# Retention and softplus feed-forward on one core: the second pass's second layer by the seven-product scheme, its out weights' sums earlier, and the order of a group's state sums kept by GpSimd

## Chip, cores and metric

One core of a Trainium2 chip. The metric is the device time of one execution in microseconds; before the change the median of three runs is 844.63 us (844.49 to 847.51).

## What is computed

Retention over 8 batches, 8 heads, 576 positions and 64 features, then a feed-forward layer over the 4608 tokens, all in float32:

```python
scores = scale * np.matmul(q, k.transpose(0, 1, 3, 2))
ret = scores * Dmat[None, :, :, :]            # Dmat: gamma_h ** (i - j) for i >= j, else 0
x = np.ascontiguousarray(attn_out.transpose(0, 2, 1, 3)).reshape(B * S, H * D)      # 4608 x 512
h = x @ w_in                                  # 512 x 2048
g = np.maximum(h, 0.0) + np.log1p(np.exp(-np.abs(h)))
return (g @ w_out).astype(np.float32)         # 2048 x 512
```

## The kernel before, in words

Every float32 product of the feed-forward is made of three TensorE products of parts (a head and a rest, `TERMS`, line 54): each operand is split by a ScalarE copy into its head and a VectorE subtraction into its rest.

The 4608 tokens are nine units of 512. Unit 0 is worked in the opening, which also splits the weights. Then come four passes over two units each (units 1 and 2, 3 and 4, 5 and 6, 7 and 8), counted in the code by `s` from 0 to 3, and called here the first to the fourth pass. The 2048 hidden features are 16 pieces of 128 or 8 pairs `J` of pieces.

- **First layer.** In passes two to four, and for pairs 6 and 7 of the first, two units and two pieces are one 2x2 block product by the Strassen-Winograd scheme: seven block products (`product`, line 820, six matmuls each; matmul line 830) in place of eight. The sums of weights that it needs (`sums_dram`) are made in the first pass. The rest of the first pass is plain: `plain_slot` (line 836), 12 slots `p` for unit 1 and 12 for unit 2, each with 12 matmuls of line 830 and 12 of the second layer.
- **Second layer.** `FULL = 2` (line 62): in the first two passes it is plain (`output_mm`, line 482: 12 matmuls for each piece of each unit, 384 in a pass). The second unit's hidden values are parked in DRAM (`kept`) and worked after the pairs (`kept_parts`). In the third and fourth pass the second layer goes by seven products too: `full_pair` (line 1129) makes two of them beside the first layer (`second`, line 1113, six matmuls at line 1117), and `full_phase` (line 1221) the other five after the eighth pair, 8 x 6 matmuls each: 336 in a pass.
- **Out weights' sums.** For these, eight pairs of out weights are added up (`whole_out`, line 625: two VectorE additions of 128x512), combined (`combine_out`, line 631: four VectorE operations of 128x256), split (`combine_split`: two ScalarE copies, two VectorE subtractions) and stored (1 MB). Pairs 0 to 6 go through this in the second pass's pairs (`extras`), pair 7 in the third pass. The raw out weights are stored in the second pass's kept part (lines 1088 to 1090).
- **Ring.** All weights of `product` and `second` come from DRAM through a ring of five 256 KB buffers (`block_load`, line 588, order in `order`, line 576). Each product frees one and issues the load of the fifth block after it. All DMAs are issued by SyncE (SP), in program order.
- **Retention.** Two steps of 128 tokens at a time (a group) are put into the slots and pairs: `chunk_products` (line 303) issues up to 128 small matmuls in four batches (`together`): state sums with t = 0 beside scores, scores beside values, values beside the cross products, and the cross products beside the state sums with t = 1. Both halves of the state sums write the same PSUM bank (`third`) from two row groups of TensorE. That the first half is done before the second begins is ensured by `mark` (line 336): a VectorE copy of one column of the first half, on which the second half waits.
- **GpSimd** scales the loaded values of the next group (`scale_values`, line 197, after the DMA `qv`), copies and scales the state (lines 259 and 278), and makes the sums of x for the next pass (`start_combined`, lines 434 to 437: four operations of 128x256) in slots 3, 5, 7 and 9 of unit 1 and 6, 8, 10 and 11 of unit 2. Groups stand in slots 0, 2, 4, 6, 8 of unit 1, in pairs 6 and 7, in the odd slots of unit 2, and in all pairs of passes two and three.

The program's order is that of the code on each engine; tables of numbers (`schedule` and `job`) put the preparations into slots and pairs. In a full pair the jobs of pair J run on VectorE in pair J + 1 (`last_difference`), after the split of its first hidden block and before the group's masking.

## Time and profile before

| | |
|---|---|
| median of 3 runs | 844.63 us |
| the profiled execution | 844.79 us |
| its span, first to last instruction | 843.0 us |
| TensorE matmuls busy | 829.7 us (98%) |
| VectorE, ScalarE, GpSimd busy | 602.4, 536.2, 157.5 us |
| DMA engines' mean busy share, rate | 72.6%, 242 GB/s |

A matmul's busy time is modelled and overlaps the next; so six matmuls of a product are shown as 1.52 us, although the next product starts 1.36 us after them. A break is therefore about 0.16 us longer than the idle time that a row shows. VectorE rows tell what each operation takes, and in square brackets what ended an idle time before it.

### The profile page before, as it was taken

Reading aid. Unit: us, or ns where it says so; the run is one execution under the profiler, and the core shown is the slowest. Engines: PE = TensorE matmul, PEld = TensorE weight load, DVE = VectorE, ACT = ScalarE, POOL = GpSimd, SP = SyncE. Lnnn points to the kernel's source line nnn. Section 1 sums busy time; section 2 is a strip of 40 time slices with the busy share of each in tenths; the row PEclk is TensorE's granted clock in tenths of the full one; section 3 lists DMA queues with packets and bytes.
Section 4 is the critical chain, followed back from the end, with each engine's and each line's share of the span. In section 5 each row is a group of like instructions: output and inputs, shape, how many; then the busy total and the mean of one; then the engine's idle time right before and its main releaser. Section 6 shows DMA issues by size and latency. Waiting matters only on the chain.

```text
span 843.0 us, 18984 instructions
## 1 busy us (share of the span) xinstructions
PE 829.7 (98%) x7370; PEld 674.8 (80%) x7370; DVE 602.4 (71%) x1024; ACT 536.2 (64%) x921; POOL 157.5 (19%) x212
## 2 busy tenths in 40 slices
PE   7999999999999999999999999999999999999998
PEld 6788888887888888888888888787778888888786
DVE  5999965876587667777775744877789955555875
ACT  6778754447654447667766436676775658878643
POOL 4322222440222441111101000112110002212100
PEclk9999999999999999999999999999999999999999
DMA  9898878656677763988789747879756676666665
GB/s 364 299 304 307 289 259 311 224 197 225 227 258 261 253 206 105 325 277 268 252 282 305 271 176 243 255 218 302 226 155 213 209 243 191 188 192 194 198 205 190
DMA packets 137481, 203.64 MB, mean 242 GB/s; under 512 B 10288, under 2 KB 99888, under 8 KB 137392
## 3 DMA queue, kind: packets, MB, share of 16 engines
q1 hardware_dynamic: 137392, 202.43, 72.6%
q8 instruction: 59, 0.97, 0.5%
q14 instruction: 30, 0.25, 0.1%
HBM read 156.25 MB, written 46.14 MB: 240 GB/s over the span
## 4 chain that ended last, share of the span: by engine, by line
PE 85%; DVE 5%; ACT 4%; DMA 3%; issue 1%; POOL 1%; SPq 0%; DVEq 0%; POOLq 0%; ACTq 0%
PE y L482 23%; PE acc L830 18%; PE sum L1117 12%; PE two L830 11%; PE h L453 4%; PE third L830 4%; PE third L220 2%; PE two L204 2%; PE two L1117 1%; PE two L282 1%; PE third L1117 1%; PE acc L1117 1%; DMA ring<-combined 1%; PE two L294 1%; DMA raw<-whole 1%
## 5 line engine op out<-in xcount | busy, mean ns | idle before, releaser
L482 PE MATMUL y<-wout,g 128*128 128x512 f32 x960 | 233.7, 392 | 0.2 <-DVE g L475 0.2
L482 PEld LDWEIGHTS y<-wout,g 128*128 128x128 f32 x960 | 178.5, 188 | 38.7 <-PE h L453 0.6
L830 PE MATMUL acc<-xt,ring 128*128 128x512 f32 x768 | 194.1, 391 | 0.4 <-DMA ring<-combined 0.2
L830 PEld LDWEIGHTS acc<-xt,ring 128*128 128x128 f32 x768 | 143.6, 188 | 32.7 <-ACT parts L1107 0.7
L830 PE MATMUL two<-xt,ring 128*128 128x512 f32 x480 | 122.4, 391 | 1.3 <-DVE quad L956 0.5
L1117 PE MATMUL sum<-parts,ring 128*128 128x512 f32 x480 | 118.1, 396 | 0.0
L830 PEld LDWEIGHTS two<-xt,ring 128*128 128x128 f32 x480 | 89.6, 188 | 22.0 <-ACT ab L1154 1.6
L1107 ACT CAST parts<-g 128x512 fp32r<-128x512 f32 x112 | 68.5, 621 | 60.0 <-PE sum L1117 19.4
L1117 PEld LDWEIGHTS sum<-parts,ring 128*128 128x128 f32 x480 | 89.1, 188 | 21.7 <-DMA ring<-outsplit 0.6
L1111 DVE TENSOR_TENSOR parts<-g,parts 128x512 fp32r<-128x512 f32 x112 | 78.0, 714 | 29.9 <-ACT parts L1107 28.6
L462 ACT ACTIVATE ab<-ab 128x512 f32<-128x512 f32 x128 | 81.0, 632 | 4.1
L463 ACT ACTIVATE ab<-ab 128x512 f32<-128x512 f32 x128 | 80.9, 632 | 4.1
L471 ACT CAST g<-ab 128x512 fp32r<-128x512 f32 x60 | 37.1, 619 | 57.5 <-DVE ab L467 35.8
L197 POOL TENSOR_TENSOR qv<-qv,consts_sb 128x256 f32<-128x256 f32 x61 | 45.7, 749 | 125.5 <-DMA qv<-others 125.5
L475 DVE TENSOR_TENSOR g<-ab,g 128x512 fp32r<-128x512 f32 x60 | 44.2, 737 | 16.2 <-ACT g L471 15.3
L259 POOL COPY sx<-s 64x256 f32<-64x256 f32 (+1 forms) x34 | 13.2, 389 | 207.6 <-PE third L220 161.2
L1127 DVE SCALAR_TENSOR_TENSOR g<-g,ab 128x512 f32<-128x512 f32 x64 | 45.2, 716 | 7.3 <-ACT ab L463 7.1
L453 PE MATMUL h<-xt,win 128*128 128x512 f32 x192 | 48.3, 400 | 1.0 <-DVE x L397 0.7
L278 POOL TENSOR_TENSOR s<-s,consts_sb 128x256 f32<-128x256 f32 (+1 forms) x31 | 20.3, 656 | 127.8 <-DVE s L276 111.7
L453 PEld LDWEIGHTS h<-xt,win 128*128 128x128 f32 x192 | 35.4, 188 | 9.6 <-ACT wout L563 0.8
L1213 POOL TENSOR_TENSOR g<-g 128x512 f32<-128x512 f32 x9 | 12.3, 1369 | 151.2 <-DVE g L1127 151.2
L461 ACT ACTIVATE ab<-quad 128x512 f32<-128x512 f32 x40 | 25.2, 631 | 23.4 <-DVE quad L956 12.0
(182 smaller groups left out, 1322.5 us busy)
## 6 DMA issues: line engine op xcount, KB each, us to landing
ring<-split SPq DMA_DIRECT2D x126, 256.0 KB, 3.9
ring<-combined SPq DMA_DIRECT2D x104, 256.0 KB, 3.6
qv<-others SPq DMA_DIRECT2D x61, 320.0 KB, 4.8
wst<-w SPq DMA_DIRECT2D x32, 512.0 KB, 5.8
ring<-outcombined SPq DMA_DIRECT2D x64, 256.0 KB, 3.4
keys<-others SPq DMA_DIRECT2D x61, 256.0 KB, 4.8
ring<-outsplit SPq DMA_DIRECT2D x48, 256.0 KB, 3.8
split<-win SPq DMA_DIRECT2D x16, 512.0 KB, 6.5
```

The source lines that it names most:

```text
L197: nc.gpsimd.tensor_mul(v, v, f.unsqueeze(2).broadcast_to([P, 4, D]))
L453: nc.tensor.matmul(h, wins[p][:, a, kt * P:(kt + 1) * P], xt[:, b, T1 + kt // 2, kt % 2], start=(n == 0), stop=(n == 3 * NKT - 1))
L462: nc.scalar.activation(ab, ab, AF.Exp, scale=-1.0)
L463: nc.scalar.activation(ab, ab, AF.Ln, bias=1.0)
L471: nc.scalar.copy(g[:, HI], ab)
L475: nc.vector.tensor_sub(g[:, LO], ab, g[:, HI].bitcast(F32))
L482: nc.tensor.matmul(ys[u][tt], g[:, a, tt * P:(tt + 1) * P], wouts[p][:, b], start=(p == 0 and n == 0), stop=(p == NF - 1 and n == 2))
L830: nc.tensor.matmul(bank, w[:, ta, kt * P:(kt + 1) * P], xt[:, tb, x, kt], start=start and k == 0, stop=k == 5, skip_group_check=True)
L1107: nc.scalar.copy(t[:, HI], g_slot(J, n))
L1111: nc.vector.tensor_sub(t[:, LO], g_slot(J, n), t[:, HI].bitcast(F32))
L1117: nc.tensor.matmul(bank[m], w[:, a, m * P:(m + 1) * P], t[:, b], start=start and n == 0, stop=n == 2, skip_group_check=True)
L1127: nc.vector.scalar_tensor_tensor(c, c, 0.0, ab, op0=ALU.max, op1=ALU.add)
```

## The change

- `FULL = 1`: the second pass goes by `full_pair` and `full_phase` too. What was the second pass's plain second layer, its parking of hidden values and its output rows are gone; the outputs of units 3 to 8 are stored swapped. The swapped layout on the host's side follows `WHOLE_TOKENS`.
- The out weights' sums: pairs 0 and 1 in the first pass's pairs 6 and 7, pairs 2, 3 and 4 in unit 2's slots 4 to 11 (in the SBUF places of out weights that are no longer needed, `whole_in`), pairs 5, 6 and 7 as jobs of the second pass. The raw out weights are stored in unit 1's slots 5, 7, 9, 11 and unit 2's slots 1, 3, 5, 7.
- The `mark`: no VectorE copy, but a GpSimd memset of one column, ordered by hand after the first half's last matmul and before the second half's first.
- The split of one x block (B22) for the third pass moves from the kept part into the first pair.

```diff
-FULL = 2
+FULL = 1
...
+        halves = [], []
...
         together((sums_mm, steps), (scores_mm, steps))
-        if steps and _chunk_kind(steps[0] // 2)[0] != HC:
-            mark = later["mark"].tile([P, 1], F32, tag="mark", name="mark")
-            nc.vector.tensor_copy(mark, third[:, 0, 0:1])
+        if halves[0]:
+            mark = nc.gpsimd.memset(later["mark"].tile([P, 1], F32, tag="mark", name="mark"), 0.0).ins
+            tc.add_manual_dep(mark, halves[0][-1].name, ordered, reason="one bank's first row group")
         together((scores_mm, steps), (values_mm, done))
         together((values_mm, done), (cross_mm, done))
         together((cross_mm, done), (sums_mm, steps))
+        if halves[0] and halves[1]:
+            tc.add_manual_dep(halves[1][0], mark.name, ordered, reason="one bank's second row group")
...
+    def raw_store(j):
+        for p, n in ((2 * j, 2 * P), (2 * j + 1, 4 * P)):
+            nc.sync.dma_start(wout_dram[p][:, :, 0:n].bitcast(F32), wouts[p][:, :, 0:n].bitcast(F32))
+
+    def whole_in(j, at):
+        whole_out(j, [wout_pools[p].tile([P, 2, T], F32, tag=f"w{p}", name="sums") for p in (2 * at, 2 * at + 1)])
...
+        *[(5 + 2 * j, raw_store, j) for j in range(4)])
...
-    extras = {(FULL - 1, J): J for J in range(NJ - 1)}
+    extras = {(0, NJ - 2): 0, (0, NJ - 1): 1}
...
+                (9, half_x, B21, STAGE[1, 0], whole, nc.vector), *[(2 * j - 7, raw_store, j) for j in range(4, NJ)],
+                (4, whole_in, 2, 0), (6, combine_out, 2), (7, split_out, 2), (8, store_out, 2),
+                (8, whole_in, 3, 1), (8, combine_out, 3), (9, split_out, 3), (10, store_out, 3),
+                (10, whole_in, 4, 2), (10, combine_out, 4), (11, split_out, 4))
...
-            last = NJ - 1
-            job(0, lambda: whole_out(last, spare[:2]))
-            job(1, combine_out, last)
-            job(2, lambda: combine_split(raws["out", last]))
-            job(3, queue_store, last)
+            for at, f, *args in ((0, whole_in, 5, 4), (0, combine_out, 5), (1, split_out, 5), (1, queue_store, 5),
+                                 (2, whole_in, 6, 5), (2, combine_out, 6), (3, split_out, 6), (3, queue_store, 6),
+                                 (3, lambda: whole_out(7, spare[:2])), (4, combine_out, 7), (5, split_out, 7),
+                                 (5, queue_store, 7)):
+                job(at, f, *args)
...
-        else:
+        if s > FULL:
             job("x", half_x, B22, STAGE[1, 1], whole, nc.vector)
```

Line numbers below are those of each kernel: 830, 482 and 1117 before are 837, 489 and 1140 in the changed one.

TensorE in the second pass, behind the first pair's group of small matmuls (`acc` and `two` are PSUM banks of the first layer's products). Before:

```order
L482 MATMUL y_3218<-wout_957,g 128x512 x3
L482 MATMUL y_3219<-wout_957,g 128x512 x3
L830 MATMUL acc<-xt,ring 128x512 x6
L830 MATMUL two<-xt,ring 128x512 x6
L482 MATMUL y_4362<-wout_175,g 128x512 x3
L482 MATMUL y_4363<-wout_175,g 128x512 x3
L830 MATMUL two<-xt,ring 128x512 x6
```

The same place in the changed kernel (`sum` is a bank of the second layer):

```order
L1140 MATMUL sum<-parts,ring 128x512 x6
L837 MATMUL acc<-xt,ring 128x512 x6
L837 MATMUL two<-xt,ring 128x512 x6
L837 MATMUL acc<-xt,ring 128x512 x6
L837 MATMUL two<-xt,ring 128x512 x6
L837 MATMUL acc<-xt,ring 128x512 x6
L837 MATMUL two<-xt,ring 128x512 x6
L1140 MATMUL sum<-parts,ring 128x512 x6
```

The plain second layer's matmuls (`y`), which stood between the products, are gone; two blocks of the seven-product second layer stand in each pair instead.

GpSimd in unit 1, from slot 4's group to slot 6's (`qv` the values of the next group, `quad` the sums of x, `sx` the state's copy). Before:

```order
L197 TENSOR_TENSOR qv<-qv,consts_sb 128x256 x2
L434 TENSOR_TENSOR quad<-xs 128x256
L435 TENSOR_TENSOR quad<-xs,quad 128x256
L436 TENSOR_TENSOR quad<-xs 128x256
L437 TENSOR_TENSOR quad<-xs,quad 128x256
L259 COPY sx<-s 64x256
```

In the changed kernel:

```order
L198 TENSOR_TENSOR qv<-qv,consts_sb 128x256 x2
L441 TENSOR_TENSOR quad<-xs 128x256
L442 TENSOR_TENSOR quad<-xs,quad 128x256
L443 TENSOR_TENSOR quad<-xs 128x256
L444 TENSOR_TENSOR quad<-xs,quad 128x256
L340 MEMSET mark 128x1
L260 COPY sx<-s 64x256
```

The mark now stands behind the four sums of x in GpSimd's order; the second half of the group's state sums on TensorE waits for it.

VectorE in unit 2, slot 10 and the group of slot 11. Before:

```order
L442 TENSOR_TENSOR xt<-quad,xt 128x8x128
L336 COPY mark<-third 128x1
L266 TENSOR_TENSOR u<-third,s 128x256
L267 TENSOR_TENSOR sx<-third,s 64x256
L276 TENSOR_TENSOR s<-third,u 128x256
```

In the changed kernel:

```order
L449 TENSOR_TENSOR xt<-quad,xt 128x8x128
L636 TENSOR_TENSOR sums<-wout_950 128x512
L636 TENSOR_TENSOR sums<-wout_951 128x512
L646 TENSOR_TENSOR sums<-sums 128x256
L647 TENSOR_TENSOR sums<-sums 128x256
L648 TENSOR_TENSOR sums<-sums 128x256
L649 TENSOR_TENSOR sums<-sums 128x256
L267 TENSOR_TENSOR u<-third,s 128x256
L268 TENSOR_TENSOR sx<-third,s 64x256
L277 TENSOR_TENSOR s<-third,u 128x256
```

Six operations for pair 4's out weights stand ahead of the state's three, and the mark is gone from VectorE.

## Rows read from the trace of the kernel before

**Rows 1.** The page: busy time of each engine, its share of the span, instructions.
```profile
PE 829.7 (98%) x7370; PEld 674.8 (80%) x7370; DVE 602.4 (71%) x1024; ACT 536.2 (64%) x921; POOL 157.5 (19%) x212
```

**Rows 2.** Busy time by stage: unit 2; the second pass; the third pass. Columns: stretch, its length, then busy us and instructions of each engine, granted clock, DMA share, GB/s.
```profile
230.18:320.17 89.99, 89.99 (x1073) 74.61 (x1073) 65.19 (x115) 42.57 (x68) 32.76 (x41) 1.00 0.71 236
320.17:501.79 181.62, 181.56 (x1682) 150.04 (x1680) 126.50 (x217) 114.21 (x187) 18.05 (x30) 1.00 0.77 261
501.79:683.47 181.68, 179.60 (x1610) 144.64 (x1608) 139.42 (x232) 119.02 (x201) 19.40 (x27) 1.00 0.71 224
```

**Rows 3.** TensorE's timeline: the end of the second pass, the leftover of it in the third pass's first pair, the last three products of the third pass. Columns: start, us, engine, line, operation, count.
```profile
456.75 45.20 PE L482 MATMUL y<-wout,g 128*128 128x512 f32 x198
...
509.95 5.60 PE L482 MATMUL y<-wout,g 128*128 128x512 f32 x24
515.39 1.52 PE L830 MATMUL acc<-xt,ring 128*128 128x512 f32 x6
...
650.05 33.58 PE L1117 MATMUL sum<-parts,ring 128*128 128x512 f32 x144
```

**Rows 4.** TensorE's timeline: the breaks of over 0.2 us idle behind the opening (one more, of 0.48 at 201.30, is in the first pass's pair 6), with the idle time and what ended it.
```profile
150.80 0.39 PE L220 MATMUL third<-qv,keys 64*64 64x64 f32 x6 [0.41 <-DVE mark L336]
527.90 0.47 PE L830 MATMUL two<-xt,ring 128*128 128x512 f32 x1 [0.40 <-ACT ab L1154]
563.84 0.27 PE L220 MATMUL third<-qv,keys 64*64 64x64 f32 x1 [0.41 <-DVE mark L336]
588.24 0.70 PE L830 MATMUL two<-xt,ring 128*128 128x512 f32 x2 [0.36 <-DMA ring<-combined]
595.20 0.21 PE L294 MATMUL two<-qv,s 64*64 64x64 f32 x1 [0.74 <-issue]
```

**Rows 5.** What TensorE waited for, in the whole span: us in total, times, longest.
```profile
PE acc L830 <- DMA ring<-combined: 0.2, 1, 0.2
```

**Rows 6.** SP's timeline in the third pass: the store of pair 7's out-weight sums and the loads behind it.
```profile
577.70 1.07 SPq L658 DMA_DIRECT2D outcombined<-quad  x2
578.95 2.30 SPq L156 DMA_DIRECT2D keys<-others  x1
581.34 0.74 SPq L600 DMA_DIRECT2D ring<-combined  x1
```

**Rows 7.** GpSimd's timeline in unit 1, up to the state's copy of slot 6's group.
```profile
161.06 1.18 POOL L434 TENSOR_TENSOR quad<-xs 128x256 f32<-128x256 f32 x1
162.32 1.60 POOL L435 TENSOR_TENSOR quad<-xs,quad 128x256 f32<-128x256 f32 x1
...
164.74 0.73 POOL L437 TENSOR_TENSOR quad<-xs,quad 128x256 f32<-128x256 f32 x1
```

**Rows 8.** VectorE and TensorE at the same place.
```profile
161.57 1.75 DVE L442 TENSOR_TENSOR xt<-quad,xt 128x1024 fp32r<-128x1024 f32 x1
164.12 0.15 DVE L336 COPY mark<-third 128x1 f32<-128x1 f32 x1
...
164.32 0.27 PE L220 MATMUL third<-qv,keys 64*64 64x64 f32 x1
```

**Rows 9.** Groups of instructions: count, then busy us, mean ns of one, idle us before.
```profile
L1364 POOL MEMSET const-float32-0.0<- 128x1 f32 x1 | 0.1, 98 | 0.3 <-issue 0.3
L629 DVE TENSOR_TENSOR quad<-wout 128x512 f32<-128x512 f32 x16 | 10.3, 686 | 0.0
L639 DVE TENSOR_TENSOR quad<-quad 128x256 f32<-128x256 f32 x16 | 8.1, 506 | 0.0
L650 DVE TENSOR_TENSOR quad<-quad 128x512 fp32r<-128x512 f32 x32 | 23.4, 771 | 0.1
```

**Rows 10.** VectorE's timeline in pair 6 of the first pass.
```profile
203.28 0.69 DVE L467 SCALAR_TENSOR_TENSOR ab<-quad,ab 128x512 f32<-128x512 f32 x1 [0.83 <-ACT ab L463]
205.78 0.69 DVE L979 TENSOR_TENSOR quad<-two,quad 128x512 f32<-128x512 f32 x1 [1.81 <-PE two L830]
207.76 0.69 DVE L987 TENSOR_TENSOR quad<-acc,quad 128x512 f32<-128x512 f32 x1 [1.29 <-PE acc L830]
```

**Rows 11.** Slots 10 and 11 of unit 2: VectorE's, GpSimd's and TensorE's timelines.
```profile
303.42 1.57 DVE L442 TENSOR_TENSOR xt<-quad,xt 128x1024 fp32r<-128x1024 f32 x1
305.16 0.16 DVE L336 COPY mark<-third 128x1 f32<-128x1 f32 x1 [0.17 <-PE third L220]
306.67 0.42 DVE L266 TENSOR_TENSOR u<-third,s 128x256 f32<-128x256 f32 x1 [1.35 <-PE third L220]
310.15 0.69 DVE L475 TENSOR_TENSOR g<-ab,g 128x512 fp32r<-128x512 f32 x1 [0.36 <-ACT g L471]
...
302.72 1.19 POOL L437 TENSOR_TENSOR quad<-xs,quad 128x256 f32<-128x256 f32 x1
306.66 0.39 POOL L259 COPY sx<-s 64x256 f32<-64x256 f32 x1 [2.75 <-PE third L220]
...
304.41 0.27 PE L220 MATMUL third<-qv,keys 64*64 64x64 f32 x1
306.44 13.90 PE L482 MATMUL y<-wout,g 128*128 128x512 f32 x60
```

**Rows 12.** GpSimd's and TensorE's timelines in unit 2, slots 6 and 7.
```profile
276.70 1.20 POOL L437 TENSOR_TENSOR quad<-xs,quad 128x256 f32<-128x256 f32 x1
...
277.95 0.27 PE L220 MATMUL third<-qv,keys 64*64 64x64 f32 x1
```

More of the change, by code (lines that the diff above doesn't have):

```diff
@@ L131, in retention_softplus_ffn @@
     place_weights(wpool, WOUT1)
+    ordered = mybir.DependencyInfo(mybir.DependencyClass.Sync, mybir.DependencyReason.DATA)
     live = {}
@@ L219, in sums_mm @@
         if follows if t else start != HC:
-            nc.tensor.matmul(L["T"][rows[h], t, part[s]], L["kp"][rows[t], s, rows[h]], L["v"][rows[t], s, rows[h]],
-                             start=True, stop=True, skip_group_check=True)
+            return nc.tensor.matmul(L["T"][rows[h], t, part[s]], L["kp"][rows[t], s, rows[h]],
+                                    L["v"][rows[t], s, rows[h]], start=True, stop=True, skip_group_check=True).ins
     def sums(m, bank):
@@ L330, in together @@
                                 clear = (j == s == 0,) if f is values_mm else ()
-                                f(which[j], s, t, h, *clear)
+                                product_of = f(which[j], s, t, h, *clear)
+                                if product_of is not None:
+                                    halves[t].append(product_of)
         together((sums_mm, steps), (scores_mm, steps))
-        if steps and _chunk_kind(steps[0] // 2)[0] != HC:
-            mark = later["mark"].tile([P, 1], F32, tag="mark", name="mark")
-            nc.vector.tensor_copy(mark, third[:, 0, 0:1])
+        if halves[0]:
+            mark = nc.gpsimd.memset(later["mark"].tile([P, 1], F32, tag="mark", name="mark"), 0.0).ins
+            tc.add_manual_dep(mark, halves[0][-1].name, ordered, reason="one bank's first row group")
         together((scores_mm, steps), (values_mm, done))
@@ L899, in prepare_store, with split_out, store_out @@
         combine_store(sums_dram[j], raws.pop(j))
+    def raw_store(j):
[3 more added lines that the diff above has]
+        whole_out(j, [wout_pools[p].tile([P, 2, T], F32, tag=f"w{p}", name="sums") for p in (2 * at, 2 * at + 1)])
+    def split_out(j):
+        combine_split(raws["out", j])
+    def store_out(j):
+        combine_store(outs_dram[j], raws.pop(("out", j)))
     def queue_store(j):
@@ L934, in retention_softplus_ffn @@
         (9, finish_combined, 2, nc.vector), (10, prepare_split, 4), (10, prepare_sums, 5), (10, half_b22, 3),
-        (11, prepare_store, 4), (11, finish_combined, 3, nc.vector), (11, prepare_head, 5))
+        (11, prepare_store, 4), (11, finish_combined, 3, nc.vector), (11, prepare_head, 5),
+        *[(5 + 2 * j, raw_store, j) for j in range(4)])
     starts = schedule(*[(3 + 2 * i, start_combined, i) for i in range(CPU)])
@@ L1056, in retention_softplus_ffn @@
                 *[(8 + 2 * i, finish_combined, i, nc.vector) for i in range(2)],
-                (9, half_x, B21, STAGE[1, 0], whole, nc.vector))
+                (9, half_x, B21, STAGE[1, 0], whole, nc.vector), *[(2 * j - 7, raw_store, j) for j in range(4, NJ)],
+                (4, whole_in, 2, 0), (6, combine_out, 2), (7, split_out, 2), (8, store_out, 2),
+                (8, whole_in, 3, 1), (8, combine_out, 3), (9, split_out, 3), (10, store_out, 3),
+                (10, whole_in, 4, 2), (10, combine_out, 4), (11, split_out, 4))
             starts = schedule(*[(min(6 + 2 * i, 2 * first - 1), start_combined, i) for i in range(CPU)])
@@ L1087, in retention_softplus_ffn @@
                 prepare_store(stores.pop(0))
-            if s == FULL - 1:
-                nc.sync.dma_start(wout_dram[2 * J][:, :, 0:2 * P].bitcast(F32), wouts[2 * J][:, :, 0:2 * P].bitcast(F32))
-                nc.sync.dma_start(wout_dram[2 * J + 1].bitcast(F32), wouts[2 * J + 1].bitcast(F32))
+            if n == 0:
+                store_out(4)
             kept_parts(u2, J, kept[n], 1)
```

## The prediction

> **What bounds the kernel now.** I read the page's busy times first: matmuls are busy 98% of the span [rows 1], so the time is TensorE's matmuls and the few breaks between them. Then the table by stage: the second pass takes 181.62 us and the third 181.68 [rows 2], although the third does its own second layer with 48 matmuls fewer. The granted clock is 1.00 of full speed, that is 2.4 GHz, in all three stages of that table [rows 2], so only count, spacing and breaks matter. Spacing comes from TensorE's timeline [rows 3]: 198 plain second-layer matmuls in 45.20 - 0.16 = 45.04 us are 0.2275 each; 144 seven-product ones in 33.58 - 0.16 = 33.42 us are 0.2321 each. So the scheme saves 384 x 0.2275 - 336 x 0.2321 = 87.4 - 78.0 = 9.4 us in a pass at best, not 48 matmuls' 10.9. The breaks I take from the rows with an idle time before them [rows 4, 5], each 0.16 longer than shown.
>
> **The second and third pass.** The changed second pass runs what the third runs today: full pairs with groups, then the phase. The nearest row is therefore the third pass itself, and I take it twice.
>
> - The second pass goes from 181.62 to 181.68: +0.06. Its first pair still holds 24 matmuls left over from unit 2, as the third's does now.
> - The third pass loses its 24 leftover matmuls: 515.39 - 509.95 = 5.44 us [rows 3].
> - Breaks in the copied pass. The one at 563.84 waits for VectorE's mark, 0.41 + 0.16 = 0.57; VectorE no longer holds the mark, so it goes from both copies: -1.14. The ones by a late ring load (588.24: 0.36 + 0.16 = 0.52; a short one just before it, at most 0.2 idle, counted 0.28 [rows 4, 5]) follow the 1 MB store of pair 7's sums at 577.70, behind which an issue stood 2.30 us [rows 6]. The 0.57 at 527.90 names a ScalarE operation that this product doesn't read, and I count it to the ring too, behind the stores of four output rows. Both causes move from the third pass to the second, so these 1.37 are paid once, not twice: -1.37. The 0.90 at 595.20 has no releaser; I keep it once: -0.90.
>
> So far 0.06 - 5.44 - 1.14 - 1.37 - 0.90 = **-8.8 us**, close to the 9.4 by counting.
>
> **What is moved into these passes.** Two pairs of out weights more (5 and 6) are prepared in the second pass. VectorE's work for one: two additions of 686 ns, four operations of at most 506, two subtractions of 771: 4.9 us [rows 9]. VectorE is busy 139.42 of 181.68 in the third pass [rows 2], and 9.8 more make 149.2 of 181.7: it fits on average. What a late masking would hold up is the next pair's second product; I price it at nothing, since VectorE no longer carries the mark, where such lateness ended on TensorE. Without that cover it is up to 0.6 a break, as at 563.84. Their two stores of 1 MB are the same as pair 7's, so each gets its price, 0.28 + 0.52 = 0.80: **+1.6** (bounds 0 and 3.2).
>
> **Unit 1.** The mark's break at 150.80 (0.57) goes. At slot 6 it grows: the mark on VectorE ends at 164.27 and TensorE goes on at 164.32 [rows 8]; on GpSimd it stands behind the four sums of x, whose last ends at 164.74 + 0.73 = 165.47 [rows 7]; a memset of one column takes 0.10 [rows 9], so TensorE goes on at 165.62, 1.30 later. Together **+0.7** (bounds -0.6, if GpSimd is on time, and 2).
>
> **The first pass's pairs 6 and 7** get the preparation of pairs 0 and 1. In pair 6, 4.9 us of VectorE's work stand against 0.83 + 1.81 + 1.29 = 3.9 us of idle time ahead of its three operations there [rows 10]. The last of them frees the bank of the last product, so TensorE waits about the difference: **+0.8** with what ScalarE hides (bounds 0 and 2). Pair 7 has longer stretches of the plain second layer between its products; nothing there.
>
> **Unit 2** gets pairs 2 to 4: 14.8 us on VectorE's 65.19 of 89.99 [rows 2], less six marks. The tight place is slots 10 and 11. VectorE ends the x split at 304.99; 1.37 + 2.02 us of pair 4 follow, so the state's operations begin at 308.38 and not at 306.67, 1.71 late [rows 11]. Slot 11's last split ends at 310.15 + 0.69 + 1.71 = 312.55; TensorE wants it after 24 of the 60 matmuls that began at 306.44, at 311.90: **+0.6** (bounds 0 and 3). Four raw stores (768 KB each) and three of sums (1 MB each) add 6.3 MB in its 90 us, 70 GB/s on 236: 306, more than the 261 that the second pass carries without such breaks [rows 2]. I price it at nothing, since a plain slot takes only two ring blocks; without that cover it is the second rival.
>
> **Sum:** -8.8 + 1.6 + 0.7 + 0.8 + 0.6 = -5.1 us. The profiled execution took 844.79 us, 0.16 above the median of 844.63; from the median it gives **839.5 us**.
>
> **Rivals.**
>
> - *The covers hold (0.20).* Stores fall between loads, and VectorE's additions into idle time: 844.6 - 8.8 = about 835.5. For it: in the second pass now, the seven such stores of pairs 0 to 6 leave no break [rows 4]. Against: those pairs take seven ring blocks each, a full pair nine.
> - *GpSimd's chain is late in unit 2 (0.20).* The next group's values are scaled when their load lands, then come the four sums of x, and only then the mark. In slot 7 the sums end at 277.90, and the mark is wanted at 277.95 + 1.5 (three of four batches), a spare of 1.5 us; in slot 11 they end at 303.91 and the mark is wanted at 305.9, a spare of 2.0 [rows 11, 12]. Two stores of 512 KB ahead of a load may cost 2.5 us, and one of the sums took 1.60 where another took 0.73, beside a VectorE split of 1.75 that otherwise takes less [rows 7, 8, 11]. With 2.5 + 1 us against each spare, 2.0 + 1.5 = 3.5 us more: 843.0. The Trainium skill (GPSIMD Engine Reference, Key points) says that GpSimd shares its SBUF interfaces with VectorE and contends with instructions that have two SBUF inputs; by that rule, every operation that the change adds to VectorE here slows the chain, and 843 would be the likelier end.
> - *Every mark comes late (0.05), the slower end.* TensorE's fourth batch waits for the mark in 25 groups. In slot 11 the four batches take 306.44 - 304.41 = 2.03 us, so the fourth begins at 305.93; VectorE's mark ends at 305.32: 0.6 to spare [rows 11]. If GpSimd answers over 0.6 us later than VectorE, each group loses the rest; from 0.37 us beyond it the kernel is slower than before by over 0.5% (25 x 0.37 = 9.3 = 5.1 + 4.2). At 0.4 beyond, 849.5. Against it: GpSimd's copy at 306.66 and VectorE's addition at 306.67 start together behind the same matmuls [rows 11].
> - *It doesn't save what it says (0.03):* 844.6. TensorE's order of instructions speaks against it.
>
> **How the numbers follow.** My sum gets 0.52, its own range 837.5 to 841.5. A measurement tells about 0.5% from no change: faster means below 840.4, slower above 848.9. Faster: about 0.36 of the first case, the 0.20 of held covers, 0.02 of the late chain: 0.58. Slower: 0.06. The rest, 0.36, is the same. The range reaches from 1 us under the first rival, 834.5, to 844.0, which takes in the late chain and leaves out the slower end, the last rival and the tails.
>
> **What would show it.** 576 plain second-layer matmuls for 960, and 816 seven-product ones for 480. The second pass about 183 us and the third about 174. No break by a VectorE mark; one by GpSimd at slot 6 of unit 1, about 1.5 us. One or two ring breaks behind the stores of pairs 5 and 6. The forecast is wrong if the second pass takes over 186 us (VectorE or the ring then bounds it), if unit 2 grows by over 2 us, or if many groups show a break at the second half of their state sums.

## The result and the profile after

The changed kernel takes 850.18 us (median of 8 runs, 846.44 to 853.16) where the kernel before takes 845.03 beside it: 1.0053 times as long, 95% interval 1.0035 to 1.0071. It is slower by about 4.5 us by the ratio (5.2 by the medians), where 5.1 less was forecast. The profiled execution took 850.67 us with a span of 848.9. The page's first row, to be held against [rows 1]:

```profile
PE 827.3 (97%) x7322; PEld 665.6 (78%) x7322; DVE 643.0 (76%) x1067; ACT 547.7 (65%) x947; POOL 165.3 (19%) x239
```

TensorE is busy 2.4 us less and the span is 5.9 us longer: the scheme saves its matmuls (48 fewer), and more than that is lost in breaks. Busy time by stage, as in [rows 2]: unit 2, the second pass, the third.

```profile
233.57:326.00 92.43, 90.89 (x1074) 74.52 (x1074) 77.90 (x133) 45.26 (x75) 35.93 (x47) 1.00 0.89 312
326.00:515.45 189.45, 182.38 (x1657) 144.26 (x1656) 151.88 (x247) 122.75 (x207) 24.12 (x39) 1.00 0.71 232
515.45:690.01 174.56, 173.53 (x1586) 139.81 (x1585) 134.19 (x217) 117.36 (x197) 18.54 (x33) 1.00 0.72 223
```

The clock is 1.00 again. Unit 2 is 2.4 us longer than before, the second pass 7.8 longer, the third 7.1 shorter. TensorE's timeline shows where: these are its larger breaks behind the opening, with the idle time and what ended it (columns as in [rows 4]).

```profile
166.51 0.27 PE L221 MATMUL third<-qv,keys 64*64 64x64 f32 x1 [1.44 <-POOL mark L340]
228.47 0.50 PE L837 MATMUL acc<-xt,ring 128*128 128x512 f32 x1 [0.99 <-DVE quad L1008]
243.17 0.27 PE L221 MATMUL third<-qv,keys 64*64 64x64 f32 x1 [0.76 <-POOL qv L198]
301.15 0.50 PE L837 MATMUL third<-xt,ring 128*128 128x512 f32 x1 [0.52 <-DVE s L277]
353.38 0.47 PE L837 MATMUL two<-xt,ring 128*128 128x512 f32 x1 [0.83 <-DMA ring<-combined]
360.44 0.21 PE L295 MATMUL two<-qv,s 64*64 64x64 f32 x1 [0.66 <-issue]
382.96 0.47 PE L837 MATMUL acc<-xt,ring 128*128 128x512 f32 x1 [0.45 <-DMA ring<-combined]
406.01 0.21 PE L295 MATMUL two<-qv,u 64*64 64x64 f32 x1 [0.64 <-issue]
417.18 0.50 PE L1140 MATMUL sum<-parts,ring 128*128 128x512 f32 x1 [0.29 <-DMA ring<-outsplit]
432.99 0.50 PE L1140 MATMUL sum<-parts,ring 128*128 128x512 f32 x1 [0.82 <-DMA ring<-outsplit]
439.68 0.21 PE L295 MATMUL two<-qv,s 64*64 64x64 f32 x1 [1.86 <-issue]
459.00 0.50 PE L1140 MATMUL two<-parts,ring 128*128 128x512 f32 x1 [0.80 <-DVE parts L1134]
465.46 0.50 PE L1140 MATMUL two<-parts,ring 128*128 128x512 f32 x1 [0.61 <-DVE parts L1134]
571.85 0.27 PE L295 MATMUL two<-qv,s 64*64 64x64 f32 x1 [0.52 <-issue]
```

Three of them, in the second pass's pairs 1, 4 and 6, and one in the third pass's pair 3 name no releaser ("issue"), like the one at 595.20 in [rows 4]. What they have in common is not in these rows, but in the list of DMA packets and in the built program. The instructions of TensorE (a matmul is a weight load and a multiplication, a float32 one twice that, and waits count too) are loaded through a queue of their own:

```profile
q8 instruction: 58, 0.95, 0.5%
```

58 packets of 16,384 bytes for 15,071 instructions, about one for each 256. Counted along the program, each of these breaks ends at place 193 or 194 of 256, and each 1.3 to 1.45 us after such a packet has landed:

```
break ends   beyond usual   place mod 256   packet starts, lands    landed to end
595.20 (before)   0.91          193          592.95   593.91           1.29
360.44            0.82          193          357.64   358.99           1.45
406.01            0.80          193          403.66   404.65           1.36
439.68            2.02          193          437.07   438.30           1.38
571.85            0.68          194          569.36   570.51           1.34
```

TensorE stands at the edge of a block of code that has not arrived. A group of small matmuls takes 256 instructions in 2 us, where products take as many in 29 us, so a late block shows inside groups. All time of TensorE, put together from the starts of its matmuls (a break is what goes beyond the usual spacing by over 0.15 us; "late code" ends at a block's edge within 0.3 us of 1.37 behind a packet's landing; the list of packets gives start and duration):

| us | before | changed |
|---|---|---|
| opening, up to the first product | 122.1 | 123.6 |
| large matmuls at their spacing | 654.2 | 647.5 |
| groups at their spacing | 56.5 | 56.8 |
| late code | 1.1 | 4.7 |
| late DMA loads | 1.1 | 3.4 |
| behind VectorE | 2.9 | 5.3 |
| behind GpSimd | 0 | 2.5 |
| other breaks | 0.6 | 0.8 |
| tail | 4.5 | 4.3 |
| span | 843.0 | 848.9 |

The work fell by 6.4 us. The breaks rose from 5.7 to 16.7. The opening's 1.5 us lie ahead of everything that the change touches (the first loads landed later in this execution); without them the span grew by 4.4, near the 4.5 of the ratio.

### The profile page after: what moved, and what is told of

Read it like the earlier page. It is cut to its first block, busy times and chain, and to the rows that moved or that the text cites. A ratio compares the mean times of both kernels' runs of the same rounds, so it can differ in the third digit from the quotient of the medians.

```text
span 848.9 us, 19021 instructions
## 1 busy us (share of the span) xinstructions
PE 827.3 (97%) x7322; PEld 665.6 (78%) x7322; DVE 643.0 (76%) x1067; ACT 547.7 (65%) x947; POOL 165.3 (19%) x239
## 4 chain that ended last, share of the span: by engine, by line
PE 76%; DVE 9%; DMA 7%; ACT 4%; issue 2%; POOL 1%; SPq 1%; DVEq 0%; ACTq 0%; POOLq 0%
PE sum L1140 19%; PE acc L837 16%; PE two L837 10%; PE y L489 10%; PE h L460 4%; PE third L837 3%; DMA ring<-outsplit 2%; PE acc L1140 2%; PE third L1140 2%; PE two L1140 2%; PE third L221 2%; PE two L205 1%; DMA qv<-others 1%; DMA ring<-combined 1%; PE two L283 1%
## 5 line engine op out<-in xcount | busy, mean ns | idle before, releaser
L1140 PE MATMUL sum<-parts,ring 128*128 128x512 f32 x720 | 178.0, 397 | 1.6 <-DMA ring<-outsplit 1.3
L1130 ACT CAST parts<-g 128x512 fp32r<-128x512 f32 x168 | 102.9, 621 | 91.7 <-DVE g L1150 30.7
L1140 PEld LDWEIGHTS sum<-parts,ring 128*128 128x128 f32 x720 | 132.8, 188 | 35.7 <-DMA ring<-outsplit 4.5
L1134 DVE TENSOR_TENSOR parts<-g,parts 128x512 fp32r<-128x512 f32 x168 | 117.7, 718 | 40.5 <-ACT parts L1130 38.1
L489 PE MATMUL y<-wout,g 128*128 128x512 f32 x576 | 140.6, 393 | 0.5 <-DVE g L482 0.5
L489 PEld LDWEIGHTS y<-wout,g 128*128 128x128 f32 x576 | 107.0, 188 | 24.2 <-DVE g L482 0.7
L1150 DVE SCALAR_TENSOR_TENSOR g<-g,ab 128x512 f32<-128x512 f32 x96 | 67.7, 718 | 7.3 <-ACT ab L470 7.1
L468 ACT ACTIVATE ab<-g 128x512 f32<-128x512 f32 x72 | 45.1, 626 | 0.0
L482 DVE TENSOR_TENSOR g<-ab,g 128x512 fp32r<-128x512 f32 x44 | 31.3, 712 | 15.0 <-ACT g L478 14.4
L221 PEld LDWEIGHTS third<-qv,keys 64*64 64x64 f32 x776 | 27.4, 134 | 13.5 <-issue 9.1
```

The lines of the kernel that those rows point to most:

```text
L221: return nc.tensor.matmul(L["T"][rows[h], t, part[s]], L["kp"][rows[t], s, rows[h]], L["v"][rows[t], s, rows[h]], start=True, stop=True, s ...
L468: nc.scalar.activation(ab, h, AF.Abs)
L489: nc.tensor.matmul(ys[u][tt], g[:, a, tt * P:(tt + 1) * P], wouts[p][:, b], start=(p == 0 and n == 0), stop=(p == NF - 1 and n == 2))
L1130: nc.scalar.copy(t[:, HI], g_slot(J, n))
L1134: nc.vector.tensor_sub(t[:, LO], g_slot(J, n), t[:, HI].bitcast(F32))
L1140: nc.tensor.matmul(bank[m], w[:, a, m * P:(m + 1) * P], t[:, b], start=start and n == 0, stop=n == 2, skip_group_check=True)
```

## The experiments

Fifteen kernels ran. "Changed" stands for the changed kernel without further edits; ratios are to the kernel before, run beside each.

| run | median us | ratio (95%) |
|---|---|---|
| changed | 850.18 | 1.0053 (1.0035 to 1.0071) |
| e1 mark on VectorE | 859.64 | 1.0168 (1.0137 to 1.0199) |
| e7 mark alone, in the kernel before | 845.38 | 1.0010 (0.9995 to 1.0024) |
| e2 code shifted | 852.65 | 1.0094 (1.0066 to 1.0122) |
| e15 code shifted, in the kernel before | 850.56 | 1.0065 (1.0040 to 1.0090) |
| e10 group split | 848.93 | 1.0047 (1.0032 to 1.0063) |
| e3 no stores in the second pass | 844.32 | 0.9999 (0.9975 to 1.0023) |
| e4 no preparation there | 845.38 | 1.0001 (0.9975 to 1.0027) |
| e8 fine stores, splits sooner | 859.32 | 1.0168 (1.0132 to 1.0205) |
| e9 fine stores, splits a pair later | 849.37 | 1.0058 (1.0037 to 1.0078) |
| e13 two stores' work earlier | 846.45 | 1.0011 (0.9995 to 1.0027) |
| e5 no raw stores | 849.20 | 1.0039 (1.0019 to 1.0060) |
| e6 VectorE for GpSimd | 846.70 | 1.0019 (0.9994 to 1.0044) |
| e11 five repairs, first choice | 848.08 | 1.0044 (1.0021 to 1.0067) |
| e12 the same, group split | 849.03 | 1.0053 (1.0034 to 1.0072) |
| e14 five repairs, second choice | 842.60 | 0.9967 (0.9953 to 0.9981) |

### The mark

**e1.** The mark back on VectorE.

```diff
-            mark = nc.gpsimd.memset(later["mark"].tile(...), 0.0).ins
-            tc.add_manual_dep(mark, halves[0][-1].name, ordered, ...)
+            nc.vector.tensor_copy(mark, third[:, 0, 0:1])
```

> The changed kernel with the mark on VectorE again, nothing else. Theory 1 (code loading: TensorE stops inside a group where its next block of instructions lands late, wherever the mark is): the breaks at the cross products of the second pass's pairs 1, 4 and 6 and the third pass's pair 3 (0.82, 0.80, 2.02 and 0.68 us) stay where they are, within 0.3 us each; only slot 6 of unit 1 changes, from 1.6 us to about 0.3, and one or two marks late by about 0.6 behind VectorE's added work come in: 848 to 850.5 against 850.2 of the changed kernel. Theory 2 (GpSimd's marks are late): those four breaks go, about 4.3 us, and with slot 6's 1.3 the kernel takes 844.5 to 845.5.

Breaks without a releaser stayed in three of the four pairs (0.82, 1.07, 0.68); the one of pair 6 went and one of 1.63 came in the third pass's pair 5. Both theories missed the total: 9.5 us slower by the medians. What TensorE waited for, and VectorE ahead of one of the worst marks (2.37 late):

```profile
PE third L221 <- DVE mark L341: 8.5, 6, 2.2
...
298.84 1.29 DVE L634 TENSOR_TENSOR sums<-wout 128x512 f32<-128x512 f32 x2
300.16 0.50 DVE L644 TENSOR_TENSOR sums<-sums 128x256 f32<-128x256 f32 x1
...
301.83 0.15 DVE L341 COPY mark<-third 128x1 f32<-128x1 f32 x1
```

On VectorE the mark stands behind the sums of pair 3 here. Behind three of the late marks the granted clock fell to one half (see e15 below): 22 large matmuls took 0.20 longer each, some 4.5 us more in this profile. Once the sums are on VectorE, the mark on GpSimd saves more than all breaks of GpSimd cost (2.5).

**e7.** The same part by itself, in the kernel before.

> The kernel before with the mark on GpSimd and nothing else changed. By the steps of the forecast: two breaks behind VectorE's mark go (0.57 each) and slot 6 of unit 1 loses 0.7 to 1.3: 844.5 to 845.5, no change. If GpSimd's marks were late in many groups, 848 to 855. The break by code loading in the third pass (0.90) stays, since TensorE's program is the same.

No change, as the steps gave it. GpSimd's marks are late in one group (slot 6 of unit 1), not in 25.

### Late code

**e2.** Instructions added where TensorE waits for the first data anyway.

```diff
+    for n in range(32):
+        nc.tensor.matmul(idle[rows[n % 2], 1, part[n % 2]], fill[rows[0], 0:HC], fill[rows[0], 0:HC], ...)
```

> The changed kernel with 32 matmuls of 64x64 more behind the opening's three idle ones: 128 instructions more on TensorE ahead of everything else, done before the first data land. Theory 1 (code loading): in the trace every such break stands at the same place of TensorE's program, instruction 193 or 194 of a block of 256, and the blocks now fall 128 instructions elsewhere in every group. The breaks in the second pass's pairs 1, 4 and 6 and the third pass's pair 3 go (under 0.2 us each); by the place of the blocks the new ones come in the second pass's pairs 0 and 5 (about 0.8), 7 (1 to 2) and perhaps 2 (0.3 to 0.6), and in the third pass's pair 4 (0.3 to 0.6). The time hardly moves: 849 to 851.5. Theory 2 (marks) or 3 (contention of transfers and engines in these pairs): the breaks stay in pairs 1, 4, 6 and 3, and the time is 850.2 within 0.5.

All four breaks went, and others came: pair 5, pair 7, the third pass's pair 4 (0.34) as worked out, pair 0 not, and two that were not foreseen, among products.

```profile
261.24 0.39 PE L489 MATMUL y<-wout,g 128*128 128x512 f32 x1 [2.80 <-issue]
...
423.05 0.21 PE L283 MATMUL two<-a,qv 64*64 64x64 f32 x1 [1.71 <-issue]
455.21 0.27 PE L221 MATMUL third<-qv,keys 64*64 64x64 f32 x2 [1.60 <-issue]
...
543.69 0.40 PE L1143 MATMUL sum<-parts,ring 128*128 128x512 f32 x1 [1.27 <-issue]
```

Each ends at place 193 of 256 again. The total missed: 852.65 lies above the expected 849 to 851.5, and late code is over 8 us in this profile, for 4.7. The other two theories fall with it: the breaks follow the program's blocks, not the marks and not what else happens in those pairs. At 261.24 the packet began 4.2 us behind the edge that stands in the group before, in a stretch whose ring loads took 5 to 7 us to land; in the second pass before, packets began 0.6 to 2.7 us behind an edge in a group.

**e15.** The same edit in the kernel before.

> The kernel before with 32 idle matmuls of 64x64 more in the opening, 128 instructions on TensorE, and nothing else. Theory 1 (code loading by the place of the blocks): in the third pass the block edges come to stand so that its break of 0.90 in pair 5 goes and others come in pairs 1, 4 and 6 (1.7, 0.8 and 1.5); 847 to 849 against 845. Rival: 845 within 0.7, the break of 0.90 stays in pair 5.

```profile
258.47 0.50 PE L482 MATMUL y<-wout,g 128*128 128x512 f32 x1 [1.81 <-issue]
541.34 0.21 PE L294 MATMUL two<-qv,sx 64*64 64x64 f32 x1 [1.82 <-issue]
```

The break of pair 5 went and pair 1's came; those of pairs 4 and 6 did not, one in unit 2 did. 32 small matmuls in idle time cost the kernel before 5.2 us by the medians, more than the changed kernel's whole loss. In this profile late code rose from 1.1 to 4.0 us; late ring loads rose too, from 1.1 to 3.4. Behind each of the two breaks above, seven large matmuls stand 0.43 us apart and not 0.23, 2.8 us together: the granted clock fell to one half there (1.2 GHz), and was full again right behind (columns as in [rows 2]).

```profile
543.00:546.20 3.20, 3.20 (x9) 2.52 (x8) 2.55 (x6) 0.00 (x0) 0.44 (x1) 0.51 0.40 138
546.30:550.00 3.70, 3.70 (x18) 3.06 (x17) 1.29 (x2) 1.93 (x4) 0.68 (x2) 1.00 0.75 257
```

This execution is the slowest of the four (853.60), so these shares are not prices by the medians, and 850.56 is above both expectations. The same fall of the clock stands behind a break in e4, e5, e6, e8, e11, e12 and e14 and behind three in e1 (breaks of 1.9 to 3.3 us), at 1.4 to 1.6 us each. The profiles of the kernel before and of the changed one have none between opening and tail: behind the changed kernel's 2.02 us at 439.68, and behind 2.96 in e2, the clock stayed at 1.00.

**e10.** One product moved into the middle of a full pair's group.

```diff
         together((scores_mm, steps), (values_mm, done))
+        if middle:
+            middle()        # product(acc, NT4), its copy, and the logs of c12
         together((values_mm, done), (cross_mm, done))
```

> The changed kernel with one product (NT4, six matmuls, 1.36 us) moved from ahead of a full pair's group into its middle, behind the second of its four batches (pairs 1 to 7 of the second and third pass). TensorE then takes 128 instructions in a row within a microsecond and not 256 within two. Theory 1 (code loading): the breaks at a block's edge inside groups of these two passes, 4.7 us together in the changed kernel, fall below 2, and the kernel takes 846.5 to 848.5, unless the masking that comes later makes a product late. Rival (the breaks belong to marks or engines): they stay at the same pairs, 850.

Late code fell from 4.7 us to none at all in this profile. The time fell by only 1.3 (0.5 by the ratios): large matmuls and groups at their spacing rose from 704.3 to 708.6 us, so changing between the two kinds twice more in 14 pairs took back 4.3 us of what was won, and 848.93 lies just above the expected 846.5 to 848.5.

Over all 17 traces, outside the stretches at half clock, 47 breaks without a releaser go beyond the usual by more than 0.25 us. All 47 end at place 193 or 194 of 256, within 0.25 us of 1.37 behind a packet's landing. The place tells where such a break can stand, not how long it is. Eight profiles have the same blocks in the second and third pass (changed, e1, e3, e4, e6, e8, e9, e13): pair 1's break is 0.6 to 0.9 us in all of them, the 2.02 of pair 6 stands in the changed kernel alone, and the third pass's pair 5 loses 0.2 us there and 0.7 to 2.4 in the other seven. With one profile of each kernel, what makes one edge late and not another is not shown.

### The stores and the preparation in the second pass

**e3, e4.** Without the three stores of sums, and without all work for pairs 5 to 7; the ring reads pair 4's sums in their place, so these outputs differ.

```diff
-... (outs_dram[j][(b - S1) // 2], b % 2)
+... (outs_dram[min(j, 4)][(b - S1) // 2], b % 2)
-    (1, queue_store, 5), (3, queue_store, 6), (5, queue_store, 7)       # e3; in e4 all rows of the list
```

> The changed kernel without the three stores of 1 MB (sums of pairs 5, 6 and 7) in the second pass; VectorE's and ScalarE's work for them stays. The ring reads pair 4's sums in their place, so as many bytes are loaded. If these stores make the second pass's ring late: the four breaks by ring loads (pair 1's 0.99, pair 2's 0.61, pairs 4 and 5's 0.46 and 0.98, 3.0 us together) fall below 0.8 together, and the kernel takes 847.5 to 848.5. If the loads of a full pair are late by themselves: all four stay, 850. The breaks inside groups stay in either case if they are code loading.

> The changed kernel without any of the preparation of pairs 5, 6 and 7 in the second pass: no additions, combining, splits and stores. The ring reads pair 4's sums in their place. Against the run without the stores alone this prices VectorE's and ScalarE's part. If VectorE's added work is hidden, as the forecast had it: within 0.6 us of that run. If it makes second products or splits late: 1 to 3 us less, 845 to 847. The 1.7 us of breaks by splits in the phase stay, since they come after these jobs, beside GpSimd's work behind the last pair.

The stores cost 5.9 us by the medians, 4.6 by the ratios, some 1.5 to 2 each; VectorE's and ScalarE's part costs nothing that can be measured. That is more than the 1.7 to 2.7 expected, and the ring's breaks did not go: in the profile of e3 late loads are 2.3 us (3.4) and late code 3.0 (4.7). Another 1.5 us lies in the spacing of the second pass's large matmuls (232.3 ns on average without the breaks, 234.5 in the changed kernel). That the stores make code late is not shown: e6 below has all three, and its code is on time in pairs 4 and 6; and in the changed kernel the late packet of pair 4 began at 403.66, ahead of pair 6's store (404.65). SP's timeline of the changed kernel at pair 5's store shows the place:

```profile
374.33 0.93 SPq L665 DMA_DIRECT2D outcombined<-sums  x2
375.32 0.98 SPq L157 DMA_DIRECT2D keys<-others  x1
377.10 0.52 SPq L607 DMA_DIRECT2D ring<-combined  x1
```

The ring block issued at 372.11 landed after 3.47 us, the one of 377.10 after 5.72, at 382.82: the break that ends at 382.96.

**e8, e9.** The stores in eight pieces, one behind each ring block.

```diff
-            queued.append(lambda where=where, f=f: combine_store([where], [f]))
+            for n in range(2):
+                for c in (slice(0, 2 * P), slice(2 * P, T)):
+                    slow.append(lambda to=where[:, n, c], x=f[:, n, c]: nc.sync.dma_start(to.bitcast(F32), x))
+        if slow: slow.pop(0)()                              # in block_load
-(1, split_out, 5) ... (3, split_out, 6) ... (5, split_out, 7)
+(0, split_out, 5) ... (2, split_out, 6) ... (4, split_out, 7)     # e8; e9: 1, 2, 5, and pair 6's sums at 1
```

> The changed kernel with each of the three stores of 1 MB in the second pass cut into eight of 128 KB, one behind each load of a ring block, in place of two of 512 KB issued together ahead of a group; the splits of pairs 5, 6 and 7 come one pair sooner for it. Without these stores the kernel took 844.3 in place of 850.2. If their price is that of a burst (late ring blocks and late code ahead of a group): the ring's breaks in pairs 2, 4 and 5 fall below 0.7 us together, and the kernel takes 846 to 848. If it is that of the bytes: 849.5 to 851.

> As the run with fine stores (each 1 MB store of the second pass as eight pieces, one behind each ring load), but with every split one pair behind its sums again, as in the changed kernel; pair 6's sums come one pair sooner to leave room. The run with fine stores lost 10 us in five breaks behind ScalarE copies that stood behind VectorE's sums, and had no ring break left behind these stores. If that placing of the splits was the cause: these five breaks go and the kernel takes 846.5 to 848.5, by the ring blocks that are on time. If the small stores themselves cost: 853 or more.

e8 was 9 us slower for a reason of its own. The split's ScalarE copy now stood right behind the sums, waited 5.21 us for VectorE, and the copy that frees TensorE's bank stood behind it:

```profile
391.95 1.14 ACT L655 CAST sums<-sums 128x512 fp32r<-128x512 f32 x2 [5.21 <-DVE sums L651]
...
395.47 0.50 PE L839 MATMUL acc<-xt,ring 128*128 128x512 f32 x1 [3.13 <-ACT g L1208]
```

e9 puts the splits back and lost those breaks, but gained nothing on the changed kernel (849.37, where 846.5 to 848.5 was expected). Smaller pieces at this place don't help.

**e13.** Pair 5 and most of pair 6 in the second pass's first pair.

```diff
-(0, whole_in, 5, 4), (0, combine_out, 5), (1, split_out, 5), (1, queue_store, 5),
-(2, whole_in, 6, 5), (2, combine_out, 6), (3, split_out, 6), (3, queue_store, 6),
+("x", whole_in, 5, 4), ("x", combine_out, 5), ("y", split_out, 5), ("y", store_out, 5),     # "x", "y":
+("y", whole_in, 6, 5), ("y", combine_out, 6), (0, split_out, 6), (0, queue_store, 6),       # inside pair 0
```

> The changed kernel with the sums of pair 5 and most of pair 6's work in the second pass's first pair, in which the DMA engines were 29% busy (88 to 95 GB/s) and VectorE 4 us of 11; pair 5's store is issued there, pair 6's one pair later and not three, pair 7's as before. If the stores cost by the fullness of the place: the ring's breaks in pairs 3 and 5 go (0.61 and 0.46), code lands earlier in pair 4 (0.80), and the kernel takes 847 to 848.5. If they cost by their bytes anywhere in this pass: 849.5 to 851.

The first pair of the changed kernel, and the same place here (columns as in [rows 2]):

```profile
326.00:343.00 17.00, 16.89 (x147) 13.30 (x148) 7.43 (x10) 9.50 (x16) 0.10 (x1) 1.00 0.29 93
```

```profile
323.97:340.97 17.00, 17.00 (x193) 14.15 (x193) 14.27 (x24) 10.45 (x19) 0.10 (x1) 1.00 0.50 160
```

3.7 us won by the medians, 3.5 by the ratios, with the same bytes and the same work (VectorE's part of it costs nothing by e4): the price was that of the place. The ring's breaks in pairs 3 and 5 went, and of the three by late code in groups of this pass only pair 1's was left (0.55); one of 0.88 came among products, one of 1.30 by a ring load in the phase, and one of 1.78 by late code in the third pass.

**e5.** Without the raw stores of units 1 and 2; the ring reads the first layer's weights in their place, so the outputs differ.

```diff
-        *[(5 + 2 * j, raw_store, j) for j in range(4)])            # and the four of unit 2
-s, n = (wout_dram[2 * j + b % 2], b // 2) if b < S1
+s, n = (split[2 * j + b % 2], b // 2) if b < S1
```

> The changed kernel without the eight raw stores (6 MB) in units 1 and 2; the ring reads the first layer's split weights in their place, as many bytes. If these stores make unit 2's loads late: the 0.92 us behind the scaling of the values in slot 1, and part of slot 6's 1.6, go, and with them up to 1 us of other lateness: 847.5 to 849. If the stores fall between loads: 850 within 0.5. The breaks in groups of the second and third pass stay within 0.5 us together (the program of TensorE is longer by one instruction, so its blocks hardly move).

About 1 us, not clear of the noise: the two intervals overlap. The wait for the scaled values in slot 1 of unit 2 stayed (0.62 and 0.89), so the raw stores were not its cause.

### GpSimd beside VectorE

**e6.** Two pieces of work from GpSimd to VectorE.

```diff
-            half_x(B12, STAGE[0, 1], slice(0, T), nc.gpsimd)
+            half_x(B12, STAGE[0, 1], slice(0, T), nc.vector)
-            engine = nc.vector if more and J < NJ - 1 else nc.gpsimd
+            engine = nc.vector if more else nc.gpsimd
```

> The changed kernel with two pieces of work given from GpSimd to VectorE: the split of the first pass's last x block in pair 7 (128x1024), beside which VectorE's two additions took 1.75 us each, and the two differences behind the second pass's last pair (128x512), beside which VectorE's splits took 0.93 to 1.8 us each. If VectorE is late there because GpSimd slows its operations (0.65 us alone): the break in pair 7 (1.15) falls below 0.5 and the two in the phase (0.96 and 0.77) below 0.9 together, 848.2 to 849.2, although VectorE gets 2.7 us more to do. If VectorE simply has too much to do there: both grow by about 1 us, 851.5 to 852.5.

In the changed kernel, pair 7 of the first pass and the phase's start, VectorE and GpSimd:

```profile
219.31 3.50 DVE L636 TENSOR_TENSOR quad<-wout 128x512 f32<-128x512 f32 x2
461.92 1.78 DVE L1150 SCALAR_TENSOR_TENSOR g<-g,ab 128x512 f32<-128x512 f32 x1
...
219.10 2.56 POOL L431 TENSOR_TENSOR xt<-xs,xt 128x1024 fp32r<-128x1024 f32 x1 [1.13 <-ACT xt L428]
461.41 1.75 POOL L1236 TENSOR_TENSOR g<-g 128x512 f32<-128x512 f32 x1
```

With GpSimd's work taken over:

```profile
218.39 1.29 DVE L636 TENSOR_TENSOR quad<-wout 128x512 f32<-128x512 f32 x2
219.60 1.22 DVE L431 TENSOR_TENSOR xt<-xs,xt 128x1024 fp32r<-128x1024 f32 x1
455.63 0.68 DVE L1150 SCALAR_TENSOR_TENSOR g<-g,ab 128x512 f32<-128x512 f32 x1
```

VectorE does the two additions and GpSimd's split in 2.4 us, where the additions alone took 3.5. Pair 7's break (1.15) and the phase's second (0.77) are gone; the first of the phase (0.95) stays, beside GpSimd's scaling of the state and the values; no repair took it away, so its cause is not shown. 3.5 us by the medians, 2.9 by the ratios, more than the 1 to 2 expected; the two breaks that went are 1.9 of it.

### Do the costs add up?

**e11, e12.** First choice of repairs: e6's, e9's stores, the first pass's last store behind the next group's loads, and the sums of x of a slot ahead of its scaling. In unit 2's last slot this forms a quarter of the second pass's sums of x ahead of the values that they need, so these outputs differ.

```diff
             states_out(*group[0])
+            for f in starts:
+                f()                    # unit 1: in slots 4, 6, 8, 10, and not 3, 5, 7, 9
```

> The changed kernel with five repairs: the two pieces of GpSimd's work on VectorE (846.7 alone), the stores of the second pass spread as in the run before, the sums of x for the third pass in unit 1 ahead of the scaling and behind a mark and not ahead of one, and the first pass's last store of sums behind the loads of the next group. Added up from the changed kernel's breaks: 3.5 for the first, 2.5 for the second, 1.0 for slot 6, 0.5 to 0.9 for slot 1 of unit 2: 842 to 843.5. If transfers and code loads only move elsewhere: 845 to 847.

> The kernel with the five repairs, and NT4 in the middle of a full pair's group. If both hold: 1.5 to 3 us less than without, 840 to 842. If code loading has no part: the same as without.

Both missed. GpSimd's breaks went (2.5 to 0), but one behind VectorE in the kept part grew from 0.4 to 2.7, with some 1.5 at half clock behind it, and late loads and late code together fell only from 8.1 to 6.7. Splitting the group gave nothing more: late code fell to 1.1, and the spacing rose by 5.3.

**e14.** Second choice: e13, e6, that store, and unit 1's marks on VectorE, where it has no sums to make.

```diff
-            chunk_products(*group)
+            chunk_products(*group, vector=u == 1)           # mark by tensor_copy there
+            if extra is not None and J == NJ - 1:           # behind the loads, in pair 7
+                combine_store(outs_dram[extra], raws.pop(("out", extra)))
```

> The run before with four repairs more, each for one break found: GpSimd's two pieces of work on VectorE (846.7 alone), the first pass's last store of sums behind the next group's loads (0.9 in slot 1 of unit 2), and unit 1's marks on VectorE again (1.6 in slot 6, less 0.6 in slot 4). Added up: 850.2 - 3.5 - 2.0 - 0.9 - 1.0 = 842.8; 841.5 to 844.5 if the costs add up, and then faster than the kernel before. 845 to 848 if late code and late ring blocks fill what is freed.

842.6, where 842.8 was added up: faster than the kernel before by 0.33% (0.19 to 0.47) and than the changed one by some 7.5 us. That the sum was met this closely is partly luck: it held 2.0 us for e13, which won 3.7; with that the sum is 841.1, so 1.5 us less was won than the parts add up to, and the first choice's sum missed by 5. Its second and third pass (columns as in [rows 2]):

```profile
321.50:504.39 182.89, 181.06 (x1657) 144.21 (x1656) 152.57 (x249) 122.01 (x207) 20.02 (x37) 1.00 0.75 240
504.39:681.93 177.54, 174.74 (x1585) 141.20 (x1584) 133.09 (x219) 117.35 (x197) 15.54 (x31) 0.99 0.70 219
```

The second pass takes the 183 us that were forecast for it; the third 3 us more than in the changed kernel. The breaks of this kernel are 10.0 us, against 16.7 and, before, 5.7: late code 3.7, late loads 1.8, VectorE 2.8, GpSimd none, others 1.7. Late code is what is left over; its largest, 1.83, stands in the third pass's pair 5. Behind it seven matmuls ran at half clock, which is 1.4 of the 1.7 and, with the break, the third pass's 3 us:

```profile
593.50:596.80 3.30, 3.30 (x9) 2.55 (x8) 3.20 (x7) 0.00 (x0) 0.02 (x1) 0.50 0.00 0
```

## Why the prediction was wrong

- **The work** was right: 576 and 816 matmuls of the two kinds, the third pass 174.6 for "about 174". Matmuls and groups fell by 6.4 us.
- **The step that failed** is "so I take it twice": the third pass's breaks were copied as if they belonged to its work. Breaks were to change by +0.3 us in all (3.4 gone, 3.7 new); they changed by +11.0. Three things lay in that:
  - *Late code.* The 0.90 at 595.20 was kept once because it "has no releaser". It was a late block of code, and where such a break can stand hangs on where blocks of 256 instructions fall (e2, e15, e10); how long it is differs from kernel to kernel at the same blocks. 0.9 became 4.3, or 4.7 with one of 0.43 that names ScalarE.
  - *The stores.* "Each gets its price, 0.80" took the breaks behind one store for its whole price. Three cost 4.6 to 5.9, since the place was full already (1.6 was added for two, 0.8 stood for the third); in pair 0 they cost less (e13). Loads behind a store there land later (5.72 us for 3.47).
  - *VectorE.* "It fits on average" held for the jobs in the pairs (e4). It failed where GpSimd works beside: pair 7 of the first pass, priced at nothing (1.15), and the phase (1.73, of which e6 took 0.77 away), which the text did not look at. Also, the third pass's last group is half a group with no state left to make; the copy has a whole one: 2.02 us on TensorE for 1.48, and three state operations on VectorE ahead of the phase's splits; no run tested this alone.
- **Unit 1** was right: slot 6's break is 1.44 idle for "about 1.5", and the stretch grew by 0.7. Pair 6 was wrong (no change for 0.8), as pair 7 was.
- **Unit 2** grew by 2.4 for 0.6, over the bound of 2 that the text had set. 0.92 was the scaling of slot 1's values, which waited for loads behind pair 1's store of sums (this wait is over 0.4 us in nine of the eleven profiles with the store ahead of the loads, 0.2 to 0.3 in the other two, and in none of the three with it behind; no run moves that store alone), 0.69 and 0.42 VectorE in slots 10 and 11. This is part of the second rival.
- **The rivals.** The slower end, every mark late, falls by e7 and e2: it gave nearly the right time, 849.5, by a mechanism that isn't there. Held covers fall too (their 844.6 - 8.8 is 835.8, not 835.5; nothing hangs on it). "GpSimd's chain is late" had the right page but looked the other way: the Trainium skill (GPSIMD Engine Reference, Key points) speaks of contention between the two engines, the forecast priced what VectorE does to GpSimd, and what cost more was what GpSimd does to VectorE (1.75 us for 0.65; 2.9 to 3.5 us of the kernel's time by e6). The trace agrees for VectorE (e6's rows).
- What stays open: how the stores' price divides, and why a block's packet is asked for so late. Where an edge fell among products of the second pass, packets began between 1.5 us ahead of it and 1.4 behind in the kernel before, 6 to 10 us behind in the changed one.

## What to carry to other kernels

A break that names no releaser is not noise to be copied: look whether it stands at a fixed place of the engine's program, and count a change's instructions for where its blocks then fall. Price a store or an engine's extra work at the place where it goes, by what the DMA engines and the other engine do there, not by an average of the pass; the same bytes cost 3.7 us less in a pair at 29% DMA. And when a pass is copied, compare its first and last pieces one by one.

## What the runs showed of the hardware

TensorE's code arrived in packets of 16 KB for 256 instructions, and TensorE stood up to 2.96 us where one came late. The Trainium skill (Runtime: NRT & Kernel Launch, Instruction fetch mechanics) gives these blocks and says that crossing one is mostly hidden; the sizes agree, and the measurement decides on the rest: 47 breaks in 17 traces. A VectorE operation on 128x512 with two inputs took 0.65 us each in pairs (1.29 for two) and up to 1.78 beside one on GpSimd. Behind twelve breaks of 1.9 to 3.3 us, in nine of the traces, the granted clock was one half (1.2 GHz) for some seven large matmuls, 0.43 us apart for 0.23; behind other breaks as long it stayed full.
